# Expert products of a float32 mixture in Strassen's form: seven block products, chunks of 768 tokens, weights streamed per chunk

## The chip, the cores and the metric

One core of a Trainium2 chip. The metric is the device time of one execution in microseconds (us), the median of several runs. All is float32. Before: 2157.72 us (3 runs, 2156.7 to 2158.68). TensorE multiplies (the profile calls it PE, and its weight loads PEld), VectorE is DVE, ScalarE is ACT, GpSimd is POOL, and SyncE (SP) issues the DMAs.

## The reference

A normed linear attention of 8 batches, 8 heads, 576 tokens and 64 head dimensions gives x of 4608 tokens by 512. Four experts then work on every token, with w1 of 512 x 1024 and w2 of 1024 x 512 each:

```python
kv = np.einsum('bhsd,bhse->bhde', k, v)
out = np.einsum('bhsd,bhde->bhse', q, kv)
out = out / np.sqrt(np.mean(out * out, -1, keepdims=True) + 1e-6) * g_norm
x = out.transpose(0, 2, 1, 3).reshape(4608, 512)
p = domain_probs / (domain_probs.sum(-1, keepdims=True) + 1e-9)
for e in range(4):
    y += p[:, e:e + 1] * (np.maximum(x @ w1[e], 0.0) @ w2[e])
```

## The kernel before

All weights stay in SBUF. Tokens go through the experts in nine chunks of 512. `up` makes 128 hidden units of one expert for all tokens of the chunk, `down` adds what they give to four PSUM sums, and `merge` (VectorE) adds an expert's share to the output by its probability, once for eight slices. The attention of the next batch is cut into pieces and woven between the slices; `attend` is the piece that matters here.

```python
def attend(b, r):                     # one block of 128 tokens
    ...                               # 4 products q @ kv into a PSUM bank, raw
    nc.scalar.activation(out=x[0:n], in_=rawh, func=ACT.Square)
    nc.vector.reduce_sum(out=ss[0:n], in_=x[0:n], axis=AX.X)
    nc.gpsimd.tensor_scalar(out=ss[0:n], ...)              # mean + eps
    nc.gpsimd.tensor_tensor(out=rt[0:n], in0=ss[0:n], in1=mhalf[0:n], op=ALU.pow)
    nc.vector.tensor_tensor(out=x[0:n], in0=rawh, in1=rt..., op=ALU.mult)

def up(c, e, fc):
    for kc in range(KC):              # 4 products of N=512
        nc.tensor.matmul(ps[:], lhsT=w1_sb[e][:, kc, ...], rhs=src[:, kc, :], ...)
    nc.scalar.activation(out=h[:], in_=ps[:], func=ACT.Relu)

def down(c, e, fc):
    for r in range(NR):               # 4 products of N=512, one PSUM bank each
        nc.tensor.matmul(o_ps[r][:], lhsT=h[:, ...], rhs=w2_sb[e][:, fc, :],
                         start=(fc == 0), stop=(fc == FCH - 1))
        if fc == FCH - 1:
            merge(c, e, r)

for slot in slots:                    # (chunk, expert, slice)
    up(*slot)
    if before: down(*before)
    if pieces and slot[1:] > (0, 3): pieces.popleft()()
    before = slot
```

## Time and profile before

| | before |
|---|---|
| median | 2157.72 us |
| first expert matmul | 59.7 us after the start |
| TensorE busy | 98%, at full clock |
| VectorE / ScalarE / GpSimd busy | 9% / 10% / 3% |
| spacing of float32 matmuls of 512 columns | 0.43 us |

The prediction below shows the lines of this profile. A busy share tells only that an engine has something to do. For TensorE the spacing of its instructions says more: a matmul's own duration (592 ns) contains pipeline that the next one overlaps.

### The profile page before, as it was taken

The page shows a single profiled execution, that of the slowest core. Times are in us where ns is not written, and L with a number is a line of the kernel's source. Part 1 is how long each engine was busy: PE and PEld are TensorE (multiplying, and loading weights), DVE is VectorE, ACT ScalarE, POOL GpSimd, SP SyncE. Part 2 cuts the span into 40 slices and gives each one's busy share as a digit, 9 for nine tenths or more (in the row PEclk, how much of TensorE's full clock was granted, in tenths as well). Part 3 has the DMA queues.
Part 4 walks back from the last instruction along what each step waited for, and adds up shares of the span by engine and source line. Part 5 has one row for each costly group of instructions (what it writes and reads, how often), then busy time and mean ns, then how long its engine had stood idle before and what let it go on. Part 6 is the DMA issues. An engine that isn't in the chain of part 4 may idle for free.

```text
span 2155.6 us, 13617 instructions
## 1 busy us (share of the span) xinstructions
PE 2118.0 (98%) x6016; PEld 990.4 (46%) x6016; DVE 197.1 (9%) x287; ACT 222.8 (10%) x369; POOL 73.9 (3%) x86
## 2 busy tenths in 40 slices
PE   4999999999999999999999999999999999999998
PEld 4444444444444444444444444444444444444443
DVE  1011000110011001110010001100111000000000
ACT  1011100110011000110011001110011000000000
POOL 1001000100000000000010000000000000000000
PEclk9999999999999999999999999999999999999999
DMA  6180003000300003000300020000200000000000
GB/s 167 30 270 0 0 0 86 0 0 0 82 5 0 0 12 75 0 0 0 86 0 0 0 71 15 0 1 5 60 0 1 20 0 0 0 20 0 0 0 20
DMA packets 64666, 55.47 MB, mean 26 GB/s; under 512 B 41056, under 2 KB 53344, under 8 KB 64608
## 3 DMA queue, kind: packets, MB, share of 16 engines
q1 hardware_dynamic: 64608, 54.61, 9.4%
q8 instruction: 47, 0.77, 0.2%
q14 instruction: 11, 0.09, 0.0%
HBM read 45.16 MB, written 9.44 MB: 25 GB/s over the span
## 4 chain that ended last, share of the span: by engine, by line
PE 98%; DMA 1%; SPq 0%; POOL 0%; DVE 0%; ACT 0%; issue 0%; ACTq 0%
PE h_ps L232 46%; PE o L246 46%; PE kv L151 2%; PE raw L181 2%; PE xT_ps L207 1%; PE qT_ps L170 1%; DMA gcol<-in_g_norm_dram 1%; POOL rt L193 0%; SPq L96 0%; DMA v<-in_v_dram 0%; DVE x L194 0%; DVE ss L188 0%; ACT x L186 0%; SPq L282 0%; SPq L99 0%
## 5 line engine op out<-in xcount | busy, mean ns | idle before, releaser
L246 PE MATMUL o<-w,h 128*128 128x512 f32 x2304 | 1035.6, 592 | 0.0
L232 PE MATMUL h_ps<-xT,w 128*128 128x512 f32 x2048 | 928.0, 596 | 0.0
L246 PEld LDWEIGHTS o<-w,h 128*128 128x128 f32 x2304 | 437.8, 190 | 551.0 <-issue 551.0
L232 PEld LDWEIGHTS h_ps<-xT,w 128*128 128x128 f32 x2048 | 379.3, 190 | 431.1 <-issue 428.2
L237 ACT ACTIVATE h<-h_ps 128x512 f32<-128x512 f32 x288 | 172.0, 597 | 1626.4 <-PE h_ps L232 1626.4
L259 DVE SCALAR_TENSOR_TENSOR acc<-o,p_all,acc 128x512 f32<-128x512 f32 x108 | 81.1, 751 | 808.1 <-PE o L246 799.4
L232 PE MATMUL h_ps<-x_rem,w 128*128 128x512 f32 x256 | 115.1, 592 | 0.0
L232 PEld LDWEIGHTS h_ps<-x_rem,w 128*128 128x128 f32 x256 | 48.6, 190 | 61.2 <-issue 61.2
L193 POOL TENSOR_TENSOR rt<-ss,mhalf 128x8 f32<-128x8 f32 (+1 forms) x40 | 65.4, 1635 | 3.3
L188 DVE TENSOR_REDUCE ss<-x 128x8 f32<-128x512 f32 (+1 forms) x40 | 27.4, 684 | 399.6 <-ACT x L186 399.6
L189 POOL TENSOR_SCALAR ss<-ss 128x8 f32<-128x8 f32 (+1 forms) x40 | 7.8, 196 | 1569.6 <-DVE ss L188 1569.6
L151 PEld LDWEIGHTS kv<-v,k 96*64 96x64 f32 x768 | 45.3, 148 | 28.7 <-issue 28.7
L151 PE MATMUL kv<-v,k 96*64 96x64 f32 x768 | 49.6, 237 | 7.3 <-DMA v<-in_v_dram 7.3
L181 PEld LDWEIGHTS raw<-kv_bd,qT 128*128 128x128 f32 (+1 forms) x320 | 44.2, 197 | 20.2 <-issue 19.0
L181 PE MATMUL raw<-kv_bd,qT 128*128 128x128 f32 (+1 forms) x320 | 46.9, 294 | 0.8 <-DVE qT L172 0.8
L158 DVE COPY kv_bd<-kv 64x256 f32<-64x256 f32 x16 | 6.8, 422 | 394.6 <-PE kv L151 394.5
L207 PE MATMUL xT_ps<-ident,x 128*128 128x128 f32 (+1 forms) x160 | 25.1, 283 | 17.1 <-DVE x L194 17.1
L186 ACT ACTIVATE x<-raw 128x512 f32<-128x512 f32 (+1 forms) x40 | 23.8, 596 | 151.2 <-PE raw L181 151.2
L257 DVE TENSOR_SCALAR acc<-o,p_all 128x512 f32<-128x512 f32 x36 | 27.0, 751 | 131.6 <-PE o L246 128.6
L172 DVE COPY qT<-qT_ps 128x512 f32<-128x512 f32 (+1 forms) x40 | 25.5, 637 | 137.0 <-PE qT_ps L170 137.0
L207 PEld LDWEIGHTS xT_ps<-ident,x 128*128 128x128 f32 (+1 forms) x160 | 19.6, 150 | 39.0 <-issue 19.3
L194 DVE TENSOR_TENSOR x<-raw,rt 128x512 f32<-128x512 f32 (+1 forms) x40 | 27.6, 690 | 81.4 <-POOL rt L193 81.4
(19 smaller groups left out, 75.1 us busy)
## 6 DMA issues: line engine op xcount, KB each, us to landing
w<-in_moe_w_dram SPq DMA_DIRECT2D x7, 2048.0 KB, 18.4
k<-in_k_dram SPq DMA_DIRECT2D x32, 288.0 KB, 3.4
v<-in_v_dram SPq DMA_DIRECT2D x32, 288.0 KB, 4.0
q<-in_q_dram SPq DMA_DIRECT2D x32, 256.0 KB, 5.3
out_dram<-acc SPq DMA_DIRECT2D x32, 256.0 KB, 4.4
w<-in_moe_w_dram SPq DMA_DIRECT2D x2, 1024.0 KB, 7.9
qr<-in_q_dram SPq DMA_DIRECT2D x8, 128.0 KB, 4.7
out_dram<-acc SPq DMA_DIRECT2D x8, 128.0 KB, 2.3
```

Of the source, the lines that this page charges most:

```text
L151: nc.tensor.matmul(ps[r * D:(r + 1) * D, hp, :], lhsT=kt[:, r, j, :], rhs=vt[:, r, j, :], start=(j == 0), stop=(j == KR - 1),)
L172: nc.vector.tensor_copy(out=t[:, :, 0:n], in_=ps)
L181: nc.tensor.matmul(raw[0:n, hp * P:(hp + 1) * P], lhsT=t[:, hp, 0:n], rhs=kv_bd[b % 2][:, hp, :],)
L188: nc.vector.reduce_sum(out=ss[0:n], in_=x[0:n], axis=AX.X)
L193: nc.gpsimd.tensor_tensor(out=rt[0:n], in0=ss[0:n], in1=mhalf[0:n], op=ALU.pow)
L194: nc.vector.tensor_tensor(out=x[0:n], in0=rawh, in1=rt[0:n].unsqueeze(2).to_broadcast([n, H, D]), op=ALU.mult,)
L207: nc.tensor.transpose(ps[:, kc, :], x[:, kc * P:(kc + 1) * P], ident[:n, :n])
L232: nc.tensor.matmul(ps[:], lhsT=w1_sb[e][:, kc, fc * P:(fc + 1) * P], rhs=src[:, kc, :], start=(kc == 0), stop=(kc == KC - 1),)
L237: nc.scalar.activation(out=h[:], in_=ps[:], func=ACT.Relu)
L246: nc.tensor.matmul(o_ps[r][:], lhsT=h[:, r * P:(r + 1) * P], rhs=w2_sb[e][:, fc, :], start=(fc == 0), stop=(fc == FCH - 1),)
L257: nc.vector.tensor_scalar_mul(out=acc[r][:], in0=o_ps[r][:], scalar1=prob)
L259: nc.vector.scalar_tensor_tensor(out=acc[r][:], in0=o_ps[r][:], scalar=prob, in1=acc[r][:], op0=ALU.mult, op1=ALU.add,)
```

## The change

The intent is to do less arithmetic on TensorE, which is the bound. A product of 2x2 blocks is made with seven block products in place of eight (Strassen's scheme in Winograd's order): sums and differences of blocks are formed first, and the products are then added up. A chunk has now 768 tokens (six chunks), and a group is 512 hidden units of one expert (eight groups a chunk, 48 in all). Weights are no longer kept in SBUF: each group's w1 and w2 are loaded again for every chunk. The forms of weights are made by GpSimd, the forms of x and h by VectorE. Cut to its core:

```diff
+    def form_w1(g):                  # w2 likewise, with right_forms
+        left_forms(nc.gpsimd, a11, a12, a21, a22, s[:, 0], s[:, 1], s[:, 2], s[:, 3])
+    def form_x(c):                   # once a chunk: four ops of 768 columns
+        right_forms(nc.vector, b11, b12, b21, b22, t[:, 0], t[:, 1], t[:, 2], t[:, 3])
...
+    ORDER = (1, 2, 6, 5, 7, 4, 3)
+    BANK = {1: 1, 6: 1, 7: 1, 4: 1, 5: 2, 3: 2, 2: 3}     # one PSUM buffer each
+    def up(g, qd, m):                # two products of N=384 into BANK[m]
+        if m in (1, 6, 7): ...       # ScalarE keeps a copy of the running sum
+        if m == 2: plus(nc.vector, h[1][:], ps, snap.pop(1)[:]); relu(h[1])
+        elif m == 7: plus(nc.vector, h[4][:], u_bank[2]..., snap.pop(7)[:]); relu(h[4])
+        elif m == 4: ...             # ScalarE: relu into h[2]
+        elif m == 3:
+            plus(nc.vector, a21[:], ps, snap.pop(6)[:])
+            relu(a21)
+            left_forms(nc.vector, h[1]..., h[2]..., a21[:], h[4]..., h[5]..., h[6]..., h[7]..., h[3]...)
+    def down(g, t, m):               # two products of N=256 into BANK[m]
+        ...
+        merge(c, e, ...)             # VectorE, after EVERY product
...
+        for g in range(total + 1):
+            if g % NG == 0 and g: form_x(g // NG)
+            ups = [(g, qd, m) for qd in range(2) for m in ORDER]
+            downs = [(g - 1, t, m) for t in range(HB) for m in ORDER]
+            load_w1(g + 1); load_w2(g)
+            # steps: 14 ups, after the nth of them the downs up to 21 * n // 14
+            for n, (what, args) in enumerate(steps):
+                what(*args)
+                if n == 4: form_w1(g + 1)
+                if n == 10: form_w2(g)
+                if pieces and n % 4 == 3: pieces.popleft()()
```

More of the change, by code (lines that the diff above doesn't have):

```diff
@@ L46 @@
     KC = DM // P
-    FCH = F // P
-    NCH = B + 1
+    NBLK = B * NR + B // 2
+    CB = 6
+    HB = CB // 2
+    NH = HB * P
+    NCH = NBLK // CB
+    GF = 512
+    GPE = F // GF
+    NG = E * GPE
     KR = 6
@@ L51 @@
     EPS = 1e-6
-    assert H * D == DM == NT and D == 64 and P == 128 and KC == NPAIR
-    assert REM == D and REM * B == NT and KP * KR == S and KP <= P
+    assert H * D == DM == NT and D == 64 and P == 128 and KC == NPAIR == 4
+    assert REM == D and REM * 2 == P and KP * KR == S and KP <= P
+    assert NBLK == NCH * CB and B % 4 == 0
     const = ctx.enter_context(tc.tile_pool(name="const", bufs=1))
-    wpool = ctx.enter_context(tc.tile_pool(name="wpool", bufs=1))
+    wpool = ctx.enter_context(tc.tile_pool(name="wpool", bufs=2))
     inpool = ctx.enter_context(tc.tile_pool(name="inpool", bufs=1))
@@ L59 @@
     xpool = ctx.enter_context(tc.tile_pool(name="xpool", bufs=2))
-    hpool = ctx.enter_context(tc.tile_pool(name="hpool", bufs=3))
+    hpool = ctx.enter_context(tc.tile_pool(name="hpool", bufs=4))
+    tpool = ctx.enter_context(tc.tile_pool(name="tpool", bufs=2))
     opool = ctx.enter_context(tc.tile_pool(name="opool", bufs=1))
     psum_a = ctx.enter_context(tc.tile_pool(name="psum_a", bufs=2, space=bass.MemoryType.PSUM))
-    psum_h = ctx.enter_context(tc.tile_pool(name="psum_h", bufs=2, space=bass.MemoryType.PSUM))
-    psum_o = ctx.enter_context(tc.tile_pool(name="psum_o", bufs=1, space=bass.MemoryType.PSUM))
+    psum_u = ctx.enter_context(tc.tile_pool(name="psum_u", bufs=1, space=bass.MemoryType.PSUM))
+    psum_d = ctx.enter_context(tc.tile_pool(name="psum_d", bufs=1, space=bass.MemoryType.PSUM))
     ident = const.tile([P, P], F32, name="ident")
@@ L68 @@
     gcol = const.tile([P, 1], F32, name="gcol")
-    x_rem = const.tile([P, KC, NT], F32, name="x_rem")
     kv_bd = [const.tile([P, NPAIR, P], F32, name=f"kv_bd{i}") for i in range(2)]
-    NBLK = NCH * NR
     p_all = const.tile([P, NBLK, E], F32, name="p_all")
@@ L74, with p_index, load_kv @@
     inv = const.tile([P, NBLK], F32, name="inv")
-    w1_sb = [wpool.tile([P, KC, F], F32, name=f"w1_{e}") for e in range(E)]
-    w2_sb = [wpool.tile([P, FCH, DM], F32, name=f"w2_{e}") for e in range(E)]
-    keys, values, queries, queries_rem = {}, {}, {}, {}
-    def load_kv(b):
-        for hp in range(NPAIR):
-            hs = slice(2 * hp, 2 * hp + 2)
-            for kept, src, tag in ((keys, k, "k"), (values, v, "v")):
-                t = inpool.tile([KP, 2, KR, D], F32, tag=tag, bufs=2, name=f"{tag}{b}_{hp}")
-                nc.sync.dma_start(
-                    out=t[:].rearrange("p h j d -> p h (j d)"),
-                    in_=src[b, hs].rearrange("h (p j) d -> p h (j d)", j=KR),
-                )
-                kept[b, hp] = t
+    blocks = []
+    for b in range(0, B, 4):
+        blocks += [(b, r) for r in range(NR)] + [(b + 1, r) for r in range(NR)]
+        blocks += [(b + 2, r) for r in range(NR - 1)] + [(b, NR)]
+        blocks += [(b + 2, NR - 1)] + [(b + 3, r) for r in range(NR)] + [(b + 2, NR)]
+    assert len(blocks) == NBLK
+    def p_index(b, r):
+        return b * NR + r if r < NR else B * NR + b // 2
+    keys, values, queries, queries_rem = {}, {}, {}, {}
+    def load_kv(b, hp):
+        hs = slice(2 * hp, 2 * hp + 2)
+        for kept, src, tag in ((keys, k, "k"), (values, v, "v")):
+            t = inpool.tile([KP, 2, KR, D], F32, tag=tag, bufs=2, name=f"{tag}{b}_{hp}")
+            nc.sync.dma_start(
+                out=t[:].rearrange("p h j d -> p h (j d)"),
+                in_=src[b, hs].rearrange("h (p j) d -> p h (j d)", j=KR),
+            )
+            kept[b, hp] = t
     def load_q(b):
@@ L97, in load_q @@
         queries[b] = t
-        t = inpool.tile([REM, H, D], F32, tag="qr", name=f"qr{b}")
+        t = inpool.tile([REM, H, D], F32, tag="qr", bufs=2, name=f"qr{b}")
         nc.sync.dma_start(out=t[:], in_=q[b, :, NT:S, :].rearrange("h p d -> p h d"))
         queries_rem[b] = t
-    def load_w1(e):
-        n = 2 if e == 0 else 1
-        for i in range(n):
-            fs = slice(i * F // n, (i + 1) * F // n)
-            nc.sync.dma_start(
-                out=w1_sb[e][:, :, fs],
-                in_=moe_w1[e][:, fs].rearrange("(kc p) f -> p kc f", p=P),
-            )
-    def load_w2(e):
-        nc.sync.dma_start(
-            out=w2_sb[e][:], in_=moe_w2[e].rearrange("(fc p) d -> p fc d", p=P)
-        )
     def load_probs():
@@ L135, in norm_probs, with diff, plus, left_forms @@
         )
-    kv_ps, xT, qT, x_tok = {}, {}, {}, {}
+    def diff(eng, out_, a, b):
+        eng.tensor_tensor(out=out_, in0=a, in1=b, op=ALU.subtract)
+    def plus(eng, out_, a, b):
+        eng.tensor_tensor(out=out_, in0=a, in1=b, op=ALU.add)
+    def left_forms(eng, a11, a12, a21, a22, s1, s2, s3, s4):
+        plus(eng, s1, a21, a22)
+        diff(eng, s3, a11, a21)
+        diff(eng, s2, s1, a11)
+        diff(eng, s4, a12, s2)
+    def right_forms(eng, b11, b12, b21, b22, t1, t2, t3, t4):
+        diff(eng, t1, b12, b11)
+        diff(eng, t3, b22, b12)
+        diff(eng, t2, b22, t1)
+        diff(eng, t4, b21, t2)
@@ new lines, with load_w1 @@
+    w1_raw, w2_raw, w1_form, w2_form = {}, {}, {}, {}
+    def load_w1(g):
+        e, i = g % NG // GPE, g % GPE
+        t = wpool.tile([P, KC, GF], F32, tag="w1r", name=f"w1r{g}")
+        nc.sync.dma_start(
+            out=t[:], in_=moe_w1[e][:, i * GF:(i + 1) * GF].rearrange("(kc p) f -> p kc f", p=P)
+        )
+        w1_raw[g] = t
+    def form_w1(g):
+        w = w1_raw.pop(g)
+        lo, hi = slice(0, GF // 2), slice(GF // 2, GF)
+        a11, a12, a21, a22 = w[:, 0:2, lo], w[:, 2:4, lo], w[:, 0:2, hi], w[:, 2:4, hi]
+        s = wpool.tile([P, 4, 2, GF // 2], F32, tag="w1s", name=f"w1s{g}")
+        left_forms(nc.gpsimd, a11, a12, a21, a22, s[:, 0], s[:, 1], s[:, 2], s[:, 3])
+        w1_form[g] = {1: a11, 2: a12, 4: a22, 5: s[:, 0], 6: s[:, 1], 7: s[:, 2], 3: s[:, 3]}
@@ new lines, in load_w2, with form_w2 @@
+    def load_w2(g):
+        e, i = g % NG // GPE, g % GPE
+        t = wpool.tile([P, 4, DM], F32, tag="w2r", name=f"w2r{g}")
+        nc.sync.dma_start(
+            out=t[:], in_=moe_w2[e][i * GF:(i + 1) * GF, :].rearrange("(c p) d -> p c d", p=P)
+        )
+        w2_raw[g] = t
+    def form_w2(g):
+        w = w2_raw.pop(g)
+        lo, hi = slice(0, DM // 2), slice(DM // 2, DM)
+        b11, b12, b21, b22 = w[:, 0:2, lo], w[:, 0:2, hi], w[:, 2:4, lo], w[:, 2:4, hi]
+        t = wpool.tile([P, 4, 2, DM // 2], F32, tag="w2t", name=f"w2t{g}")
+        right_forms(nc.gpsimd, b11, b12, b21, b22, t[:, 0], t[:, 1], t[:, 2], t[:, 3])
+        w2_form[g] = {1: b11, 2: b21, 3: b22, 5: t[:, 0], 6: t[:, 1], 7: t[:, 2], 4: t[:, 3]}
@@ L140, in bank @@
+    xT, x_form = {}, {}
+    def form_x(c):
+        x = xT[c]
+        lo, hi = slice(0, NH), slice(NH, 2 * NH)
+        b11, b12, b21, b22 = x[:, 0:2, lo], x[:, 0:2, hi], x[:, 2:4, lo], x[:, 2:4, hi]
+        t = xpool.tile([P, 4, 2, NH], F32, tag="xt", bufs=1, name=f"xt{c}")
+        right_forms(nc.vector, b11, b12, b21, b22, t[:, 0], t[:, 1], t[:, 2], t[:, 3])
+        x_form[c] = {1: b11, 2: b21, 3: b22, 5: t[:, 0], 6: t[:, 1], 7: t[:, 2], 4: t[:, 3]}
+    kv_ps, qT, x_tok = {}, {}, {}
     def bank(name):
@@ L197, in attend, with turn_x @@
         x_tok[b, r] = x
-    def turn_x(b, r):
+    def turn_x(b, r, i):
         n = rows_of(r)
-        if r == 0:
-            xT[b] = xpool.tile([P, KC, NT], F32, tag="xT", name=f"xT{b}")
+        c, at = i // CB, i % CB * P
+        if c not in xT:
+            xT[c] = xpool.tile([P, KC, 2 * NH], F32, tag="xT", name=f"xT{c}")
+        if r == NR:
+            at += b % 2 * REM
         x = x_tok.pop((b, r))[0:n].rearrange("p h d -> p (h d)")
@@ L207, in turn_x @@
             nc.tensor.transpose(ps[:, kc, :], x[:, kc * P:(kc + 1) * P], ident[:n, :n])
-        dst = xT[b][:, :, r * P:(r + 1) * P] if r < NR else x_rem[:, :, b * REM:(b + 1) * REM]
-        nc.scalar.activation(out=dst, in_=ps, func=ACT.Copy, scale=gcol[:])
-    def attention(b):
-        pieces = [lambda hp=hp: key_values(b, hp) for hp in range(NPAIR)]
-        pieces.append(lambda: load_kv(b + 1) if b + 1 < B else None)
-        pieces.append(lambda: turn_q(b, 0))
-        for r in range(NR + 1):
-            pieces.append(lambda r=r: attend(b, r))
-            if r < NR:
-                pieces.append(lambda r=r: turn_q(b, r + 1))
-            else:
-                pieces.append(lambda: load_q(b + 1) if b + 1 < B else None)
-            pieces.append(lambda r=r: turn_x(b, r))
-        return pieces
@@ L225, with attention, load_first @@
-    hidden, o_ps, acc = {}, {}, {}
-    def up(c, e, fc):
-        src = xT[c] if c < B else x_rem
-        ps = psum_h.tile([P, NT], F32, tag="h", name=f"h_ps{c}_{e}_{fc}")
-        for kc in range(KC):
+        nc.scalar.activation(out=xT[c][:, :, at:at + n], in_=ps, func=ACT.Copy, scale=gcol[:])
+    seen = set()
+    def attention(c):
+        todo = []
+        for i in range(c * CB, (c + 1) * CB):
+            b, r = blocks[i]
+            todo += [(b, NR, i), (b + 1, NR, i)] if r == NR else [(b, r, i)]
+        order = sorted(todo, key=lambda t: (t[0], t[1]))
+        pieces = []
+        waiting = []
+        fresh = sorted({b for b, r, i in order} - seen)
+        def load_first():
+            if fresh:
+                b = fresh.pop(0)
+                pieces.append(lambda: (load_kv(b, 0), load_kv(b, 1)))
+        load_first()
+        for n, (b, r, i) in enumerate(order):
+            if b not in seen:
+                seen.add(b)
+                for hp in range(NPAIR):
+                    if hp + 2 < NPAIR:
+                        pieces.append(lambda b=b, hp=hp: (key_values(b, hp), load_kv(b, hp + 2)))
+                    else:
+                        pieces.append(lambda b=b, hp=hp: key_values(b, hp))
+                load_first()
+            pieces.append(lambda b=b, r=r: turn_q(b, r))
+            if r == NR - 1:
+                pieces.append(lambda b=b: load_q(b + 1) if b + 1 < B else None)
+            if waiting:
+                pieces.append(waiting.pop())
+            pieces.append(lambda b=b, r=r: attend(b, r))
+            waiting.append(lambda b=b, r=r, i=i: turn_x(b, r, i))
+        pieces.append(waiting.pop())
+        return pieces
@@ new lines, with keep, relu @@
+    hidden, acc, snap = {}, {}, {}
+    ORDER = (1, 2, 6, 5, 7, 4, 3)
+    BANK = {1: 1, 6: 1, 7: 1, 4: 1, 5: 2, 3: 2, 2: 3}
+    FIRST = (1, 2, 5)
+    u_bank, d_bank = {}, {}
+    def keep(name, tag):
+        return tpool.tile([P, NH], F32, tag=tag, name=name)
+    def relu(t):
+        nc.scalar.activation(out=t[:], in_=t[:], func=ACT.Relu)
+    def up(g, qd, m):
+        n = f"{g}_{qd}"
+        if m in FIRST:
+            u_bank[BANK[m]] = psum_u.tile([P, NT], F32, tag=f"u{BANK[m]}", name=f"u{BANK[m]}_{n}")
+        ps = u_bank[BANK[m]][:, 0:NH]
+        wf, xf = w1_form[g][m], x_form[g // NG][m]
+        for c in range(2):
@@ L232, in up @@
             nc.tensor.matmul(
-                ps[:], lhsT=w1_sb[e][:, kc, fc * P:(fc + 1) * P], rhs=src[:, kc, :],
-                start=(kc == 0), stop=(kc == KC - 1),
-            )
-        h = hpool.tile([P, NT], F32, tag="h", name=f"h{c}_{e}_{fc}")
-        nc.scalar.activation(out=h[:], in_=ps[:], func=ACT.Relu)
-        hidden[c, e, fc] = h
-    def down(c, e, fc):
-        h = hidden.pop((c, e, fc))
-        for r in range(NR):
-            if fc == 0:
-                o_ps[r] = psum_o.tile([P, DM], F32, tag=f"o{r}", name=f"o{c}_{e}_{r}")
-            nc.tensor.matmul(
-                o_ps[r][:], lhsT=h[:, r * P:(r + 1) * P], rhs=w2_sb[e][:, fc, :],
-                start=(fc == 0), stop=(fc == FCH - 1),
-            )
-            if fc == FCH - 1:
-                merge(c, e, r)
@@ L253, in merge, with unit @@
-    def merge(c, e, r):
-        prob = p_all[:, c * NR + r, e:e + 1]
-        if e == 0:
-            acc[r] = opool.tile([P, DM], F32, tag=f"acc{r}", name=f"acc{c}_{r}")
-            nc.vector.tensor_scalar_mul(out=acc[r][:], in0=o_ps[r][:], scalar1=prob)
+                ps, lhsT=wf[:, c, qd * P:(qd + 1) * P], rhs=xf[:, c, :],
+                start=(m in FIRST and c == 0), stop=(c == 1), skip_group_check=True,
+            )
+        h = hidden.setdefault((g, qd), {})
+        def unit(tag):
+            return hpool.tile([P, NH], F32, tag=tag, name=f"{tag}_{n}")
@@ new lines, in up @@
+        if m in (1, 6, 7):
+            snap[m] = keep(f"s{m}_{n}", f"s{m}")
+            nc.scalar.activation(out=snap[m][:], in_=ps, func=ACT.Copy)
+        if m == 2:
+            h[1] = unit("h1")
+            plus(nc.vector, h[1][:], ps, snap.pop(1)[:])
+            relu(h[1])
+        elif m == 7:
+            h[4] = unit("h4")
+            plus(nc.vector, h[4][:], u_bank[2][:, 0:NH], snap.pop(7)[:])
+            relu(h[4])
+        elif m == 4:
+            h[2] = unit("h2")
+            nc.scalar.activation(out=h[2][:], in_=ps, func=ACT.Relu)
+        elif m == 3:
+            a21 = keep(f"a21_{n}", "a21")
+            plus(nc.vector, a21[:], ps, snap.pop(6)[:])
+            relu(a21)
+            h[5], h[6], h[7], h[3] = unit("h5"), unit("h6"), unit("h7"), unit("h3")
+            left_forms(
+                nc.vector, h[1][:], h[2][:], a21[:], h[4][:], h[5][:], h[6][:], h[7][:], h[3][:]
+            )
@@ L258, in merge @@
+    def merge(c, e, i, half, ps):
+        b, r = blocks[c * CB + i]
+        prob = p_all[:, p_index(b, r), e:e + 1]
+        cols = slice(half * DM // 2, (half + 1) * DM // 2)
+        if (c, i) not in acc:
+            acc[c, i] = [opool.tile([P, DM], F32, tag=f"acc{i}", name=f"acc{c}_{i}"), set()]
+        t, made = acc[c, i]
+        if half not in made:
+            made.add(half)
+            nc.vector.tensor_scalar_mul(out=t[:, cols], in0=ps, scalar1=prob)
         else:
             nc.vector.scalar_tensor_tensor(
-                out=acc[r][:], in0=o_ps[r][:], scalar=prob, in1=acc[r][:],
@@ L261, in merge @@
-                op0=ALU.mult, op1=ALU.add,
-            )
-        if e == E - 1:
-            store(c, r)
-    def store(c, r):
-        if c < B:
-            rows = out[c * S:c * S + NT, :].rearrange("(p r) d -> p r d", r=NR)
-            nc.sync.dma_start(out=rows[:, r, :], in_=acc[r][:])
+                out=t[:, cols], in0=ps, scalar=prob, in1=t[:, cols], op0=ALU.mult, op1=ALU.add,
+            )
+    def down(g, t, m):
+        c, e = g // NG, g % NG // GPE
+        if m in FIRST:
+            d_bank[BANK[m]] = psum_d.tile(
+                [P, NT], F32, tag=f"d{BANK[m]}", name=f"d{BANK[m]}_{g}_{t}"
+            )
+        ps = d_bank[BANK[m]][:, 0:DM // 2]
+        for qd in range(2):
+            nc.tensor.matmul(
+                ps, lhsT=hidden[g, qd][m][:, t * P:(t + 1) * P], rhs=w2_form[g][m][:, qd, :],
+                start=(m in FIRST and qd == 0), stop=(qd == 1), skip_group_check=True,
+            )
+        if m in (1, 2):
+            merge(c, e, t, 0, ps)
+        elif m in (6, 3):
+            merge(c, e, t, 1, ps)
+        elif m in (5, 7):
+            merge(c, e, HB + t, 1, ps)
+        elif m == 4:
+            merge(c, e, HB + t, 0, ps)
+        if m == ORDER[-1] and g % NG == NG - 1:
+            store(c, t)
+            store(c, HB + t)
@@ L270, in store @@
+    def store(c, i):
+        b, r = blocks[c * CB + i]
+        t = acc.pop((c, i))[0]
+        if r < NR:
+            rows = out[b * S:b * S + NT, :].rearrange("(p r) d -> p r d", r=NR)
+            nc.sync.dma_start(out=rows[:, r, :], in_=t[:])
             return
         for bb in range(2):
-            end = (2 * r + bb + 1) * S
-            nc.sync.dma_start(out=out[end - REM:end, :], in_=acc[r][bb * REM:(bb + 1) * REM, :])
+            end = (b + bb + 1) * S
+            nc.sync.dma_start(out=out[end - REM:end, :], in_=t[bb * REM:(bb + 1) * REM, :])
@@ L276 @@
     with tc.manual_schedule(engines={ENG.PE, ENG.DVE, ENG.Activation, ENG.Pool, ENG.SP}):
-        load_kv(0)
+        first = attention(0)
+        first.pop(0)()
         load_q(0)
         load_w1(0)
-        load_w2(0)
         for i in range(P // D):
@@ L287 @@
             nc.vector.memset(t[:], 0.0)
-        for piece in attention(0):
+        for n, piece in enumerate(first):
             piece()
-        for e in range(1, E):
-            load_w1(e)
-            load_w2(e)
+            if n == 2:
+                load_w2(0)
+                form_w1(0)
         norm_probs()
-        slots = [(c, e, fc) for c in range(NCH) for e in range(E) for fc in range(FCH)]
+        form_x(0)
+        total = NCH * NG
         pieces = deque()
-        before = None
-        for slot in slots:
-            if slot[1:] == (0, 0):
+        for g in range(total + 1):
+            if g % NG == 0 and g < total:
+                if g:
+                    form_x(g // NG)
                 assert not pieces
-                if slot[0] + 1 < B:
-                    pieces.extend(attention(slot[0] + 1))
-            up(*slot)
-            if before:
-                down(*before)
-            if pieces and slot[1:] > (0, 3):
-                pieces.popleft()()
-            before = slot
-        down(*before)
+                if g // NG + 1 < NCH:
+                    pieces.extend(attention(g // NG + 1))
+            ups = [(g, qd, m) for qd in range(2) for m in ORDER] if g < total else []
+            downs = [(g - 1, t, m) for t in range(HB) for m in ORDER] if g else []
+            if g + 1 < total:
+                load_w1(g + 1)
+            if 0 < g < total:
+                load_w2(g)
+            steps = []
+            done = 0
+            for n, u in enumerate(ups):
+                steps.append((up, u))
+                upto = len(downs) * (n + 1) // len(ups)
+                steps += [(down, d) for d in downs[done:upto]]
+                done = upto
+            steps += [(down, d) for d in downs[done:]]
+            for n, (what, args) in enumerate(steps):
+                what(*args)
+                if n == 4 and g + 1 < total:
+                    form_w1(g + 1)
+                if n == 10 and g < total:
+                    form_w2(g)
+                if pieces and n % 4 == 3:
+                    pieces.popleft()()
+            if g:
+                for qd in range(2):
+                    hidden.pop((g - 1, qd))
 _INS = ['q', 'k', 'v', 'g_norm', 'moe_domain_probs', 'moe_w1', 'moe_w2']
```

## The prediction

> **What bounds the kernel now.** I read the page's busy shares and slices first, then the chain that ended last, then the groups, then the timeline of one woven attention block and of the first 60 us. The busy shares, the slices of TensorE and of its clock, and the chain:
>
> ```profile
> PE 2118.0 (98%) x6016; PEld 990.4 (46%) x6016; DVE 197.1 (9%) x287; ACT 222.8 (10%) x369; POOL 73.9 (3%) x86
> ...
> PE   4999999999999999999999999999999999999998
> ...
> PEclk9999999999999999999999999999999999999999
> ...
> PE 98%; DMA 1%; SPq 0%; POOL 0%; DVE 0%; ACT 0%; issue 0%; ACTq 0%
> PE h_ps L232 46%; PE o L246 46%; PE kv L151 2%; PE raw L181 2%; PE xT_ps L207 1%; PE qT_ps L170 1%; DMA gcol<-in_g_norm_dram 1%; POOL rt L193 0%; SPq L96 0%; DMA v<-in_v_dram 0%; DVE x L194 0%; DVE ss L188 0%; ACT x L186 0%; SPq L282 0%; SPq L99 0%
> ```
>
> TensorE works in every slice at full clock, 92% of the chain is the two expert products, and every other engine is nine tenths idle. A busy PE need not be PE at its peak, so I checked the rate in a window of the steady stream:
>
> ```profile
> 304.19 3.60 PE L246 MATMUL o<-w,h 128*128 128x512 f32 x8
> ```
>
> Eight instructions in 3.60 us; the last shows its own 592 ns of pipeline, so the spacing is (3600 - 592)/7 = 430 ns (the weight loads beside it start 429 ns apart). Each float32 product is two such instructions. 4608 x 0.429 = 1976 us are the experts. The rest is 60 us of start (first expert matmul below) and some 108 us of attention of seven batches woven in, all on PE. PE has no gaps left, so only fewer matmul columns help. That is what Strassen's form offers.
>
> ```profile
> 59.69 9.22 PE L232 MATMUL h_ps<-xT,w 128*128 128x512 f32 x16
> ```
>
> **What the Trainium skill says.** "TensorE: Matmul & The Clock Gate", section "Wait — 56ns, not 53.3ns?", gives the warm spacing as N/2.4 GHz plus about 2.5 ns; the trace agrees for two passes of N=512 (2 x 213.3 + 2 = 429). "VectorE: DVE Perf Modes", section on the TRN2 errata, gives (N+151)/0.96 ns for a float32 tensor_tensor; the trace's 690 ns at 512 agrees exactly. "GPSIMD Engine Reference", section "Performance versus the Vector engine", gives 4497 ns for a two-input float32 op of 2048 elements, so I estimate 1.15 us for 512; the trace before has no such op. "SBUF — State Buffer", section "Who interferes with whom", says a VectorE op with two SBUF inputs contends with a GpSimd op that reads SBUF; no run of before shows it.
>
> **The change, part by part.**
>
> *TensorE.* There are 6 chunks x 8 groups (512 hidden units each) = 48 groups. A group has 2 x 7 x 2 up products of N=384 and 3 x 7 x 2 down products of N=256, in two instructions each: 2688 instructions of N=384 and 4032 of N=256. By the spacing above that is 384/1.2 + 2 = 322 ns and 256/1.2 + 2 = 215 ns. Weight loads must not bind at the shorter N: the 128x128 products of the attention answer that.
>
> ```profile
> 163.03 1.05 PE L181 MATMUL raw<-kv_bd,qT 128*128 128x128 f32 x8
> 164.12 0.60 ACT L186 ACTIVATE x<-raw 128x512 f32<-128x512 f32 x1 [3.67 <-PE raw L181]
> 164.75 0.69 DVE L188 TENSOR_REDUCE ss<-x 128x8 f32<-128x512 f32 x1 [15.00 <-ACT x L186]
> 165.52 0.20 POOL L189 TENSOR_SCALAR ss<-ss 128x8 f32<-128x8 f32 x1 [20.45 <-DVE ss L188]
> 165.80 1.64 POOL L193 TENSOR_TENSOR rt<-ss,mhalf 128x8 f32<-128x8 f32 x1
> 167.47 0.69 DVE L194 TENSOR_TENSOR x<-raw,rt 128x512 f32<-128x512 f32 x1 [2.04 <-POOL rt L193]
> ```
>
> (1050 - 275)/7 = 111 ns per load and matmul at N=128, so loads keep up. Experts: 2688 x 0.322 + 4032 x 0.2154 = 866 + 868 = **1734 us**, 242 less than 1976; per group 36.1 us (an up step of four instructions 1.29, a down step 0.86).
>
> *VectorE and ScalarE.* Per group VectorE gets 14 ops of 384 columns ((384+151)/0.96 = 557 ns) and 21 merges of 256 columns. From the row
>
> ```profile
> L259 DVE SCALAR_TENSOR_TENSOR acc<-o,p_all,acc 128x512 f32<-128x512 f32 x108 | 81.1, 751 | 808.1 <-PE o L246 799.4
> ```
>
> a merge is 751 - 267 = 485 ns. That is about 16 us of 38, so VectorE is not full. ScalarE gets 14 ops of some 0.5 us. What counts is the order: VectorE works in program order and each PSUM bank has one buffer, so PE waits where a merge is late. From a matmul's streaming end to its reader is 0.2 us (its shown end plus 40 ns), back to PE 0.05 us. I walked one group by hand:
>
> - In the first token block, down products 7 and 4 use one bank with no up step between. The wait is 0.2 + 0.485 + 0.05 = 0.74 us.
> - After up product 3 of each half, VectorE does the sum a21 (done at 0.76), waits for ScalarE's relu (to 1.36), makes four forms (s1, s3, s2, s4, to 3.47), and only then the next merge (to 3.9). PE has a down, an up and another down to do meanwhile, 3.01 us, then needs that merge: 0.92 us lost, twice a group (the second at the start of the next).
> - Elsewhere a step or two lies between, and covers.
>
> That is 2.6 us a group, 47 x 2.6 = 122, and 4 for the first and last group, which lack the other kind of steps.
>
> *Attention.* On PE, from the timeline: turn 0.44, scores 0.89, turn 0.44 a full block, some 5.0 for a batch's key-values. 34 blocks and 6 batches are woven in: 88 us. In an attend, VectorE stands in order until the last multiply, 4.1 us after the scores end (the timeline above: 164.08 to 168.16). Before, nothing waited for VectorE; now merges stand behind it. I placed the 34 attends in the eight slots of a group from the program order (4, 4, 6, 7, 1, 4, 5, 3 of them) and worked out each slot's extra wait: 0.35, 3.0, 0.45, 2.5, 0.85, 0.3, 2.4, 2.5 us. The worst are where a merge or the forms are due at once. Sum 55 us; turns of q add some 4.
>
> *GpSimd and DMA.* GpSimd forms each group's weights in 8 x 1.15 = 9 us of 38. The weights are read six times, 2 MB a group: the kernel before moved 270 GB/s in its third slice, so about 8 us of the 38, issued a group ahead. Both are hidden. By my walk the weight forms end some 13 us into a group and VectorE's own two-input forms come at 18 and 36 us, so they rarely meet.
>
> *Start and end.* A sixth block at 7 us, a second batch's keys loaded in halves behind its predecessor's, later issue of half of batch 0's keys; less time lost to g_norm, which lands earlier as fewer bytes are ahead of it. I get the first expert matmul at some 77 us, against 59.7. Chunk borders put four forms of x before merges: 5 x 1.4 = 7. Last merge and store 6.
>
> Sum: 77 + 1734 + 88 + 122 + 4 + 55 + 4 + 7 + 6 = 2097 us. I add 13 for meetings of GpSimd and VectorE and waits my walk missed: **2110 us**, 2.2% faster. The arithmetic gain of 242 us shrinks to about 50, mostly by waits of PE for VectorE.
>
> **Rivals.**
>
> *A: PE stays the bound; waits overlap with woven work.* Then 77 + 1734 + 88 + 13 is 1912 as a floor and about 2000 with some waits. For it: VectorE is half idle. Against it: one bank buffer each and strict order, with four small ops and a relu ahead of a merge that PE needs within 3 us.
>
> *B: GpSimd and VectorE block each other.* If a weight form takes 1.5 us or more, or weights land late, the second set of weight forms reaches VectorE's forms 18 us into the group; each of four forms could wait a GpSimd op. 2 to 4 us a group is 100 to 190 us: 2200 to 2290. For it: both read two SBUF inputs. Against it: my times keep them apart.
>
> *C: weights arrive late.* 2 MB in 38 us is 55 GB/s, a fifth of what the kernel before reached. I give it little.
>
> **Range and chances.** The PE term is firm to 1%, the start to 10 us. The waits (190 us in my sum) may be a third less, or half more, and B adds a tail upward. So 2040 to 2200. The 2% border lies at 2114.6, almost at my number: faster 0.50, within 2% 0.38, slower 0.12.
>
> **What would show it.** In the profile after: matmul spacing of 322 and 215 ns (a window of few instructions); PE's idle time, about 200 us after the start, released by VectorE merges, mostly ahead of down products; VectorE near 45%, GpSimd near 25%; VectorE forms at 557 ns (longer would speak for B); waits of VectorE for GpSimd's rt near 2 us each. The first expert matmul at 77 us. I am wrong if loads bind at N=256 (spacing above 230 ns), if PE's waits name another engine, if idle time is far below 150 us, or if PE's clock falls because of the gaps.

## The result, and the profile after

The changed kernel is correct and takes 2215.41 us (median of 4 runs, 2211.17 to 2221.73), against 2157.73 us for the kernel before in the same rounds. A ratio here is the mean time of one kernel's fast runs over that of the other's of the same rounds, so not quite the ratio of the medians: 1.0269, with a 95% interval of 1.0251 to 1.0288. It is slower, and 105 us above the prediction.

The page of the kernel after: busy shares, the slices of TensorE and its clock, and the chain that ended last.

```profile
PE 1960.7 (89%) x8128; PEld 1404.9 (64%) x8128; DVE 965.0 (44%) x1847; ACT 386.2 (17%) x753; POOL 577.0 (26%) x470
...
PE   4789899888899988999988889998988998999998
...
PEclk9799999999999999999999989999999999999999
...
PE 72%; DVE 18%; POOL 3%; ACT 3%; issue 2%; DMA 1%; SPq 1%; ACTq 0%; POOLq 0%; DVEq 0%
```

TensorE's busy time fell from 2118.0 to 1960.7 us, yet the span grew: TensorE now has gaps, and 18% of the chain that sets the end lies on VectorE. The mean granted clock is 0.970, against 0.999.

To see where time goes I took the trace group by group: from a group's first up product to the next group's, less its matmuls at their spacing at full clock (322 ns for 384 columns, 215 for 256, 111 for the 128x128 scores, 109 for turns, 52 for key-values). What is left is lost time.

| | predicted us | trace us |
|---|---|---|
| start, to the first expert matmul | 77 | 75.6 |
| TensorE at full clock, experts and attention | 1734 + 88 | 1824 |
| waits that each of 47 groups has | 122 | 47 x 3.09 = 145 |
| five chunk borders, above such a group | 7 | 5 x 8.8 = 44 |
| attention, above such a group | 55 + 4 | 103 |
| first and last group's own | 4 | 13 |
| last merge and store | 6 | 5 |
| allowance | 13 | |
| sum | 2110 | 2209 (the span) |

This is the profiled execution, 2211.17 us by the device's time. The 8.8 us are from the one border that has no attention in it (group 40: 47.98 us long, against 39.21 for a steady group); the attention's 103 are what the other rows leave of the 304 us lost. Within these 304, some 43 us are not gaps at all but matmuls at half clock, counted by doubling a matmul's spacing where the trace's clock record says one half (in these stretches the median spacing measures 1.97 to 1.99 times the full one).

Most of the account was right. The waits of a steady group stand in its timeline where the prediction put them (kernel after, a group without attention; the bracket is the engine's idle time and what ended it, and pipeline of 0.16 us comes on top):

```profile
1987.11 1.13 PE L403 MATMUL d<-w2r,h 128*128 128x256 f32 x4 [0.77 <-DVE acc L391]
...
1996.24 1.10 PE L403 MATMUL d<-w2t,h 128*128 128x256 f32 x4 [0.67 <-DVE acc L391]
...
2007.63 1.13 PE L403 MATMUL d<-w2t,h 128*128 128x256 f32 x4 [0.77 <-DVE acc L391]
```

0.77 + 0.16 = 0.93 us twice, where 0.92 was predicted, and 0.67 + 0.16 = 0.83 between products 7 and 4, where it was 0.74. The other 0.4 us of the 3.09 are small delays, of 0.11 us or less each.

The border is another matter. The timeline of the kernel after at the start of group 40, VectorE forming x (xt) beside GpSimd forming weights (w1s, w2t):

```profile
1862.32 3.17 DVE L150 TENSOR_TENSOR xt<-xT 128x768 f32<-128x768 f32 x2
1862.70 1.98 POOL L150 TENSOR_TENSOR w1s<-w1s,w1r 128x512 f32<-128x512 f32 x1
...
1865.41 3.95 DVE L150 TENSOR_TENSOR xt<-xT,xt 128x768 f32<-128x768 f32 x2
1866.58 3.91 POOL L150 TENSOR_TENSOR w2t<-w2r 128x512 f32<-128x512 f32 x2
...
1869.91 2.05 PE L403 MATMUL d<-w2t,h 128*128 128x256 f32 x4 [4.57 <-DVE acc L391]
...
1871.75 2.77 PE L347 MATMUL u<-xt,w1s 128*128 128x384 f32 x4
```

Two forms of x take 3.95 us and two weight forms 3.91: each engine's op lasts some 1.96 us, though GpSimd's takes 1.27 elsewhere. The merge behind the forms comes late, TensorE stands 4.57 us, and then four matmuls of 384 columns take 2.77 us in place of 1.45: the clock has halved. An attention block can bring the same about in any group. Here (kernel after) VectorE waits for the attend's last multiply, and so makes the forms of h at the next group's start, where GpSimd forms weights:

```profile
567.92 0.69 DVE L269 TENSOR_TENSOR x<-raw,rt 128x512 f32<-128x512 f32 x1 [2.04 <-POOL rt L268]
...
570.50 1.58 POOL L150 TENSOR_TENSOR w1s<-w1s,w1r 128x512 f32<-128x512 f32 x1
570.88 1.61 DVE L150 TENSOR_TENSOR h<-h,a 128x384 f32<-128x384 f32 x1
...
572.41 3.15 DVE L150 TENSOR_TENSOR h<-h,h 128x384 f32<-128x384 f32 x2
...
576.01 2.07 PE L403 MATMUL d<-w2r,h 128*128 128x256 f32 x4 [7.17 <-DVE acc L391]
```

In a steady group the last two forms take 1.15 us together; here they take 3.15, and TensorE waits 7.17 us.

One entry of the list of waits misleads: it puts 17.7 us of TensorE's waits, in four gaps, to GpSimd's w2t. The w2t forms that the waiting matmuls read were all finished before their group began, and in each of the four a merge behind an attend ended 0.14 to 0.15 us before the matmul started. These gaps belong to the attends.

### The profile page after: what moved, and what is told of

It is laid out like the page before. It is cut to its first block, busy times and chain, and to the rows that moved or that the text cites. A ratio compares the mean times of both kernels' runs of the same rounds, so it can differ in the third digit from the quotient of the medians.

```text
span 2209.1 us, 20936 instructions
## 1 busy us (share of the span) xinstructions
PE 1960.7 (89%) x8128; PEld 1404.9 (64%) x8128; DVE 965.0 (44%) x1847; ACT 386.2 (17%) x753; POOL 577.0 (26%) x470
## 4 chain that ended last, share of the span: by engine, by line
PE 72%; DVE 18%; POOL 3%; ACT 3%; issue 2%; DMA 1%; SPq 1%; ACTq 0%; POOLq 0%; DVEq 0%
PE u L347 34%; PE d L403 33%; DVE h L150 7%; DVE acc L391 3%; DVE h L153 3%; DVE a L153 2%; ACT a L337 2%; POOL rt L268 2%; PE kv L226 2%; DVE xt L150 1%; PE raw L256 1%; PE xT_ps L285 1%; DVE ss L263 1%; DVE x L269 1%; PE qT_ps L245 1%
## 5 line engine op out<-in xcount | busy, mean ns | idle before, releaser
L391 DVE SCALAR_TENSOR_TENSOR acc<-d,p_all,acc 128x256 f32<-128x256 f32 x936 | 443.1, 481 | 648.4 <-PE d L403 647.3
L403 PE MATMUL d<-w2t,h 128*128 128x256 f32 x2304 | 604.1, 390 | 135.8 <-DVE acc L391 107.9
L403 PEld LDWEIGHTS d<-w2t,h 128*128 128x128 f32 x2304 | 430.9, 193 | 301.9 <-DVE acc L391 74.1
L403 PE MATMUL d<-w2r,h 128*128 128x256 f32 x1728 | 442.5, 388 | 66.4 <-DVE acc L391 55.6
L403 PEld LDWEIGHTS d<-w2r,h 128*128 128x128 f32 x1728 | 329.3, 193 | 189.6 <-DVE acc L391 80.6
L347 PE MATMUL u<-xt,w1s 128*128 128x384 f32 x1152 | 428.4, 496 | 2.0 <-DVE xt L150 2.0
L347 PE MATMUL u<-xT,w1r 128*128 128x384 f32 x768 | 294.7, 509 | 0.0
L347 PEld LDWEIGHTS u<-xt,w1s 128*128 128x128 f32 x1152 | 224.6, 195 | 98.8 <-issue 6.3
L347 PEld LDWEIGHTS u<-xT,w1r 128*128 128x128 f32 x768 | 151.7, 199 | 66.4 <-issue 8.5
L347 PE MATMUL u<-xt,w1r 128*128 128x384 f32 x384 | 142.2, 493 | 0.6 <-ACT s L358 0.6
```

What stands on the lines that cost most here:

```text
L347: nc.tensor.matmul(ps, lhsT=wf[:, c, qd * P:(qd + 1) * P], rhs=xf[:, c, :], start=(m in FIRST and c == 0), stop=(c == 1), skip_group_check ...
L391: nc.vector.scalar_tensor_tensor(out=t[:, cols], in0=ps, scalar=prob, in1=t[:, cols], op0=ALU.mult, op1=ALU.add,)
L403: nc.tensor.matmul(ps, lhsT=hidden[g, qd][m][:, t * P:(t + 1) * P], rhs=w2_form[g][m][:, qd, :], start=(m in FIRST and qd == 0), stop=(qd ...
```

## The experiments

The theories: (1) VectorE's ops of two SBUF inputs and GpSimd's ops lock each other out where they meet, at chunk borders and behind attends; (2) attends hold VectorE for 4 us with merges behind, whatever GpSimd does; (3) a long gap costs again, as TensorE's clock halves after it. The rival to (1) is that (2) alone makes the long gaps. Another is GpSimd's own queue: its two small ops of an attend stand in order with the weight forms. The waits of the steady group are tested too. Each run changes one thing in the changed kernel, whose 2215.41 us is the base; the last ones combine. The runs were spread over three chips, on which the kernel before took 2157.0 to 2158.3 us.

| run | what is changed | us | ratio to before |
|---|---|---|---|
| (the change) | | 2215.41 | 1.0269 |
| e1_swap_pool | GpSimd: second product's weight forms first | 2170.28 | 1.0059 |
| e2_split_attend | attend's VectorE ops asked for later | 2115.31 | 0.9802 |
| e3_spread_7_4 | an up product between down products 7 and 4 | 2175.08 | 1.0088 |
| e4_late_forms | forms of h one a step, behind merges | 2079.69 | 0.9639 |
| e5_border_early | forms of x in the group before | 2177.79 | 1.0087 |
| e6_no_wforms | no weight forms (wrong result) | 2149.82 | 0.9964 |
| e7_fill | useless matmuls in the borders' gaps | 2211.25 | 1.0245 |
| e8_all | e1 to e5 | 1940.60 | 0.8991 |
| e9_swap_split | e1 and e2 | 2093.65 | 0.9702 |
| e10_all_but_swap | e2 to e5 | 1936.27 | 0.8977 |

### The lock: e1_swap_pool and e6_no_wforms

```diff
-                if n == 4 and g + 1 < total: form_w1(g + 1)
-                if n == 10 and g < total: form_w2(g)
+                if n == 4 and g < total: form_w2(g)
+                if n == 10 and g + 1 < total: form_w1(g + 1)
```

> Only the order of GpSimd's two weight forms in a group is changed: the second product's first, the first product's after it, so GpSimd starts some 4 us later in a group. Theory 1 (GpSimd and VectorE lock each other out where VectorE's two-input ops, the forms of x at a chunk border or late forms of h, meet the weight forms; the long gaps that follow also halve TensorE's clock for a while): the five borders lose about 5 us instead of 8.8 above a steady group's, the 4 to 7 us gaps ahead of the first down product of a group go, the granted clock rises from 0.97 to above 0.98, time 2215 to about 2165 us. Rival (VectorE's strict order behind the attention alone makes the gaps, the lock is a side effect): under 10 us gained, 2205 or more.

2170.28 us; the granted clock rose to 0.978, a little less than expected. The border without attention shrank from 47.98 to 40.85 us; the group after it gave 3.8 us back. The gaps of 3.4 to 7.2 us in the first 12 us of a group are gone but for three of 3.4 us, and a new one of 9.0 us stands in group 25, where VectorE waits 7.4 us for the attend's rt. The gain of 45 us is what theory 1 says; the rival is out for the borders. That attends alone still make gaps, the next run shows.

The other run takes GpSimd's ops away altogether, with raw blocks of the same shapes in the products:

```diff
-        left_forms(nc.gpsimd, a11, a12, a21, a22, s[:, 0], s[:, 1], s[:, 2], s[:, 3])
-        w1_form[g] = {1: a11, 2: a12, 4: a22, 5: s[:, 0], 6: s[:, 1], 7: s[:, 2], 3: s[:, 3]}
+        w1_form[g] = {1: a11, 2: a12, 4: a22, 5: a21, 6: a11, 7: a12, 3: a21}
```

> Wrong result on purpose: GpSimd forms no weights, the products read raw blocks of the same shapes. TensorE, VectorE, ScalarE and the loads do the same work. Theory 1: every VectorE op of two SBUF inputs goes back to its own time (0.56 us for 384 columns, 0.88 to 0.95 for 768), borders lose about 1.5 us, some 60 us are gone: 2150 to 2160 us, a little below the run with the swapped order (2170), which left a few meetings. What the attends cost alone stays. Rival (GpSimd's work costs nothing in itself): 2205 or more.

2149.82 us, with a wrong result as meant (relative error 3.4). The groups of VectorE ops by shape, first the kernel after, then this run (busy us, mean ns of one):

```profile
L150 DVE TENSOR_TENSOR xt<-xT,xt 128x768 f32<-128x768 f32 x12 | 23.5, 1957 | 0.2
```

```profile
L150 DVE TENSOR_TENSOR xt<-xT,xt 128x768 f32<-128x768 f32 x12 | 11.5, 955 | 0.2
```

The same op takes 1957 ns beside GpSimd and 955 without. "SBUF — State Buffer", section "Who interferes with whom", of the Trainium skill says that a VectorE op of two SBUF inputs and a GpSimd op that reads SBUF shut each other out, and that one with a single SBUF input does not; the merges, which read PSUM and one SBUF tensor, took 481 ns in both runs. GpSimd's weight forms so cost the changed kernel 66 us in all (2215.41 - 2149.82). GpSimd's queue is a small part of it: VectorE's waits for rt sum to 85.1 us in the kernel after and to 81.4 here. The border now costs 1.65 us above a steady group (40.80 against 39.15). What stays are the attends, with no weight form anywhere: 14 gaps of 3.2 to 3.7 us, such as this one (group 18):

```profile
861.83 0.69 DVE L265 TENSOR_TENSOR x<-raw,rt 128x512 f32<-128x512 f32 x1 [2.04 <-POOL rt L264]
862.43 0.47 DVE L387 SCALAR_TENSOR_TENSOR acc<-d,p_all,acc 128x256 f32<-128x256 f32 x1
862.96 1.65 PE L399 MATMUL d<-w2r,h 128*128 128x256 f32 x3 [3.66 <-DVE acc L387]
```

### The attends: e2_split_attend and e9_swap_split

```diff
         nc.scalar.activation(out=x[0:n], in_=rawh, func=ACT.Square)
-        (mean square, GpSimd's power, last multiply)
+        held[b, r] = ...        # mean square and power: emitted after the next step
+        finish[b, r] = ...      # last multiply: emitted in the next piece, four steps on
```

> VectorE no longer stands still in an attention block: the mean square is asked for one step later and the last multiply four steps later, in the next piece. Theory 2 (the attends, by holding VectorE some 4 us, cause most of the lost time outside steady groups, directly and by pushing VectorE's forms into GpSimd's): some 50 us of gaps and 25 us of half clock go, about 2140 us; the five chunk borders stay as they are. Rival (the lock at the borders and not the attends): 2195 or more.

2115.31 us, 100 us less where some 75 were expected, with the granted clock at 0.983. Many groups with attention now lose about what others do (group 10, for one, 2.17 us, where the kernel after lost 5.55), though some still lose 4 to 5 us and one 7.3, and the borders still lose 9.5 to 11.4. The table's row for attention falls from 103 to 11. So the attends were the larger part.

> The swapped order on GpSimd and the split attends together; alone they gave 45 and 100 us. If the attends' cost ran partly through the lock (late forms of h meeting the weight forms), the two gains overlap: less than the sum, which would be 2070 us; I expect 2075 to 2085. If they are independent: 2070 or less.

2093.65 us. Together the two give 122 us, alone 45 and 100: they overlap by 23 us. I read this as the part of the attends' cost that ran through the lock, and the other 77 (2170.28 - 2093.65) as VectorE standing in order, with what the clock adds. e6 agrees: with no weight forms at all, the table's row for attention is 83 us, 20 below the kernel after. I had expected a smaller overlap, of 5 to 15 us.

### The steady group's waits: e3_spread_7_4 and e4_late_forms

```diff
-                upto = len(downs) * (n + 1) // len(ups)
+                upto = (1, 3, 4, 5, 7, 9, 10, 12, 13, 15, 16, 18, 19, 21)[n] if downs else 0
```

> The up and down products interleave otherwise, so that an up product stands between down products 7 and 4 of the first token block. My step of 0.74 us a group (the trace shows 0.83): 47 x 0.83 = 39 us off, 2176 us, steady groups 38.4 instead of 39.2 us. If the wait only moves to the next merge: 2205 or more.

2175.08 us; steady groups take 38.26 us instead of 39.21. The step was right.

```diff
-            left_forms(nc.vector, h[1]..., a21[:], h[4]..., h[5]..., h[6]..., h[7]..., h[3]...)
+            later.append(lambda: plus(nc.vector, s1, a, a22))   # and the other three likewise
 ...
+                due = len(later)
                 what(*args)
+                if due: later.popleft()()
```

> VectorE's four forms of h are made one after each following step, behind that step's merge, instead of all four ahead of the next merge. By my step of twice 0.93 us a group, 47 x 1.86 = 87 us off: about 2128 us, steady groups 37.4 us. But the last forms of a group now fall into the next group's start, where GpSimd forms weights: if the lock matters, steady groups keep 0.5 to 1 us of it and the time is 2140 to 2170; GpSimd's ops then grow from 1.26 us to 1.5 or more.

2079.69 us, 136 us less where 87 were expected. Steady groups take 37.14 us: 2.07 us less, 97 us over 47 groups. By the two profiles, which are 130 us apart, 31 more lie in groups with attention, most likely because a merge no longer stands behind four forms as well as behind an attend. GpSimd's ops did grow, as feared (two of the first product's four forms to 1.47 us, from 1.37 and 1.38), and VectorE's last two forms to 729 ns, but nothing was waiting closely behind them, and steady groups show no cost.

### The borders: e5_border_early and e7_fill

```diff
-                if g: form_x(g // NG)          # at the chunk's first group
+                # t3 in place of its operand, so that xt fits twice
+                if g % NG == NG - 1 and n == 20: form_x(g // NG + 1)
+                if x_later and n % 3 == 2: x_later.popleft()()
```

> The forms of the next chunk's x are made in the second half of a chunk's last group, when GpSimd is idle, in a second buffer (one form in place of its operand; two snapshot tiles lose their second buffer to make room). Theory 1: the five borders lose 8.8 us each above a steady group, 44 us in all, and nearly all of it comes back: about 2173 us; the forms of x take 0.9 to 1.0 us instead of 1.7 to 2.0. Rival (borders are slow for another reason, the stores or the loads of keys): 2205 or more.

2177.79 us. The border without attention now takes 39.09 us, as any other group. The forms for the five borders take 0.95 us each, as expected; the mean over all is 1.1, since those of the first chunk still meet GpSimd (1.8 to 2.0 us). The five border groups together went from 265.8 to 229.2 us: 37 of the 5 x 8.8 us came back.

```diff
+                if n == 4 and g and g % NG == 0 and g < total:
+                    for i in range(5): nc.tensor.matmul(junk[:, 0:NH], ...)   # two instructions each
```

> The changed kernel with ten useless matmuls (3.2 us of PE, into a bank nobody reads) ahead of the product at each of the five chunk borders where TensorE stands 4.7 us. Theory 3[...]: the gap shrinks to 1.5 us, the clock stays full there, and the kernel gets FASTER by 1.7 to 3.4 us a border, 2215 to about 2203 us. Rival (the clock is read low only because TensorE idles, and costs nothing): 2215 or more, as the filling takes no time that was used.

2211.25 us, ratio 1.0245 with an interval of 1.0230 to 1.0261: lower than the change's, but the intervals overlap, so the whole does not settle theory 3. The place does. Windows over group 40, first of the kernel after, then of this run (busy us and instructions by engine, then TensorE's granted clock):

```profile
1858.50:1906.40 47.90, 39.78 (x141) 27.74 (x140) 25.01 (x40) 7.06 (x14) 12.98 (x8) 0.93 0.15 50
```

```profile
1859.20:1903.50 44.30, 40.48 (x151) 28.10 (x151) 24.03 (x40) 7.06 (x14) 13.04 (x8) 1.00 0.15 55
```

With ten more matmuls the group is 3.7 us shorter, and the clock stays full. In the kernel after, the three steps behind the gap took 2.7 us longer than at full clock; the remaining 1 us is from forms of h that did not meet GpSimd this time. The five border groups together went from 265.8 to 255.7 us. The rest of the gain was lost elsewhere: other groups were longer than in the kernel after: groups 10, 26 and 35, which have attention, by 1.7, 2.9 and 2.3 us, and the last one by 1.6. These half-clock stretches last 3.4 us or a multiple of it, and where they fall differs from run to run. "TensorE: Matmul & The Clock Gate" of the Trainium skill, section "Why this matters for your kernels", asks for no idle gaps above some 3 us between bursts, and names half rate as what follows. The traces agree on what follows, not on the bound. I counted TensorE's gaps from the first expert matmul on, in the profiles of the changed kernel and its ten variants, and whether a half-clock stretch began within 3.5 us of the gap's end:

| gap of TensorE, us | gaps | followed by half clock |
|---|---|---|
| 1.0 to 1.5 | 55 | 0 |
| 1.5 to 2.0 | 52 | 2 |
| 2.0 to 2.5 | 38 | 20 |
| 2.5 to 3.0 | 7 | 4 |
| 3.0 to 3.3 | 44 | 33 |
| 3.3 to 3.8 | 31 | 28 |
| above 3.8 | 48 | 48 |

So there is no sharp bound: the longer the gap, the more often the clock halves. In e4 one of 2.20 us did it, and in the kernel after one of 3.53 us did not.

### All together: e8_all and e10_all_but_swap

> Swapped order on GpSimd, split attends, the spread of products 7 and 4, late forms and the early border together. What stays by my sum: start 79, TensorE 1824, some 0.3 us a group, some 25 us of attends and ends: 1945 us, 10% below the kernel before. If the gains hide each other or the deferred forms now meet GpSimd: 1980 to 2020.

1940.60 us, ratio 0.8991: 10% faster than the kernel before.

> All parts of the best version but the swapped order on GpSimd: what the lock still costs where nothing waits closely behind VectorE's forms. By theory 1 the forms of h at a group's start meet the weight forms and are stretched, but no merge stands directly behind them: within 15 us of the best version's 1941, so 1941 to 1955. If the lock costs in any schedule: 1965 or more.

1936.27 us, ratio 0.8977 (0.8964 to 0.8990), the fastest of all, though the interval overlaps with e8's (0.8976 to 0.9006). Its page, busy shares and slices:

```profile
PE 1884.3 (97%) x8128; PEld 1394.6 (72%) x8128; DVE 944.9 (49%) x1847; ACT 387.5 (20%) x753; POOL 572.3 (30%) x470
...
PE   4699999999999999999999999999999999999998
...
PEclk9699999999999999999999999999999999999999
```

The same instructions on TensorE, the same work on the others, and TensorE full again: a steady group takes 36.19 us, against 36.13 of matmul. The lock is still there (VectorE's last forms of h take 730 ns, against 549 in e8), and costs nothing that shows. The swapped order of e8 gains nothing more; it is 4 us slower, nearly all of it in start and groups with attention, but it ran on another chip and a difference this small isn't settled.

## Why the prediction was wrong

Taken by its own steps:

- **TensorE's spacing and count, the start, the weights' loads: right.** 1734 + 88 was 1824, and 77 was 75.6 us. The loads landed 5 us after issue. Rival C (weights late) came about in one place: behind a border, w1's load stands behind the chunk's stores on SyncE and is issued 3.5 to 7.0 us into the group, where most others are issued 35 us or more into the group before. In group 25 the attend's power so stood behind late weight forms, and TensorE waited 6.61 us, against 3.66 in e6.
- **The steady group's waits: right in kind, a fifth too small.** 2.6 us was 3.09, 145 us in place of 122; the place of each wait was right, and e3 and e4 took them out. (The "about 16 us" of VectorE's work are 18 by the prediction's own figures, 14 x 0.557 + 21 x 0.485; nothing rests on it.)
- **"Both are hidden. By my walk the weight forms end some 13 us into a group and VectorE's own two-input forms come at 18 and 36 us, so they rarely meet": this step failed.** The walk was of a group that nothing disturbs. The weight forms start 1.5 us into a group, which the walk did not count, and there they meet two kinds of VectorE work: the forms of x at a border, and the forms of h of the group before, once an attend has pushed them back. Without the weight forms the span is 61 us shorter (e6). Rival B had the mechanism, but looked for the meeting at 18 us in every group; a steady group loses 0.06 us to it (39.21 against 39.15 in e6). That 2215 lies in B's range of 2200 to 2290 does not make B's sum right.
- **"Chunk borders ... 5 x 1.4 = 7" was mis-sized**: 44 us. It took a form of x at its own 0.9 us, where the lock made it 1.96, and had no clock in it. Without the lock it was right: 5 x 1.65 = 8 us in e6. e5 brought back 37.
- **"Sum 55 us" for the attends was mis-sized**: 103. The slots' waits were worked out one by one with VectorE alone, and with VectorE alone they were about right: of the 83 us in e6 some 26 are half clock, which leaves 57, where 55 + 4 was predicted. The other 20 of the 103 went with the weight forms, much as the overlap of 23 in e9 says.
- **TensorE's clock** was named as a sign of being wrong and given no cost. It cost some 43 us, nearly all of it inside the two items above. By this count it was 31 us without weight forms (e6), 10 with the order swapped and the attends split (e9) and 4 in e10.

So the direction of the error was in sight (the tail upward by B) and was given 0.12. The "gain shrinks by waits of PE for VectorE" was right, and the experiments show that most of these waits came from the order in which VectorE's work was emitted: the same arithmetic in another order, with buffers given out a little differently, is 279 us faster.

What stays open: how much a half clock costs in a whole run can't be set apart from the gaps that cause it; e7 shows it at one place only. Why some gaps of 2 to 3.5 us are followed by half clock and others are not stays open too.

## What to carry to other kernels

A saving on the bound engine is worth what the helpers' queues let through: where every product is followed by a small op that the next product waits for, walk each in-order queue for the worst neighbour, not the average load, and emit long or waiting work behind the short op that is urgent. Check not only whether two engines that share a port meet in an undisturbed period, but also where disturbed work is pushed to. A gap of TensorE of 2 us or more can cost twice, as the clock may halve behind it.

## What the Trainium skill lacked or had wrong

- "TensorE: Matmul & The Clock Gate": no spacing for float32. Here each float32 product is two instructions, whose spacing is 429 ns at 512 columns, 322 at 384, 215 at 256 and 111 at 128, loads included. Its formula for one pass (N/2.4 + 2.5 ns) gives these within 2 ns when N is doubled.
- "GPSIMD Engine Reference": a two-input float32 op of 512 columns has no figure; a quarter of the page's 2048-column time is 1.12 us, and the runs show 1.27 (e1, where it meets little).
- "SBUF — State Buffer": says that the shared pair is an exclusive lock, but not what comes of two queues that both need it. Here the ops seem to take turns, each beginning while the other's runs: a VectorE op of 768 columns goes from 0.955 to 1.96 us, and GpSimd's from 1.27 to 1.96. Where nothing waited closely behind VectorE's ops, stretched forms of h (730 ns, from 556) cost no time that shows (e10).
- "TensorE: Matmul & The Clock Gate": its bound of some 3 us for idle gaps is too wide for these runs, where 20 of 38 gaps of 2.0 to 2.5 us were followed by half clock, and none of 55 gaps of 1.0 to 1.5 us. The runs add that 3.2 us of useless matmuls in a 4.6 us gap kept the clock full (e7).
